# Differences of the second product beside the first one, ScalarE's parametric ReLU for the leak

## The chip, the cores and the metric

One core of a Trainium2 chip runs the whole program. The metric is the device time of one execution in microseconds (us). In the profile PE is TensorE's matmul, PEld its weight load, DVE is VectorE, ACT is ScalarE, POOL is GpSimd, and SP is SyncE, whose queue issues most DMAs.

## The reference

```python
def _attn_ref(q, k, v, p):
    # sm_attn: softmax(scale * q k^T) v
    p_packed = sm_attn(p, k, v)
    return sm_attn(q, p_packed, p_packed)
...
def _moe_ref(x, w_gate, w_val, w_out, rms_g):
    rms = np.sqrt(np.mean(x * x, axis=-1, keepdims=True) + 1e-06)
    xn = x / rms * rms_g
    g = xn @ w_gate
    silu = g * (1.0 / (1.0 + np.exp(-g)))
    return (silu * (xn @ w_val)) @ w_out
...
def _moe2_ref(x, w_in, w_out):
    h = x @ w_in
    g = np.maximum(0.01 * h, h)
    return g @ w_out
```

The three run one after the other: 8 x 8 heads of 576 x 64 with 32 packed rows; then 4608 tokens of 512, first through the gated layer (1536 wide), then through the leaky one (2048 wide). The change touches only the leaky layer.

## The kernel before

All matmuls are fp32-accurate by splitting each operand into a high and a low part: ACT copies the high part (`act_copy`), DVE subtracts it from the value for the low part (`sub`, L167), and `mm3` runs hi x hi, lo x hi and hi x lo. So a product of two operands has three matmuls, and each operand costs one ACT and one DVE instruction to split.

**The z stage.** The first 2048 tokens of the leaky layer are computed beside the second half of the attention, in 64 steps: `stage3z` multiplies by `w_in` into PSUM (`zh`), ACT makes 0.01 x h (`zr`), DVE takes the maximum (`zgf`, L1095), ACT and DVE split the result (`zgh`, `zgl`), and two steps later `stage4z` multiplies by `w_out`. `fold` (L895, `pwps`) is a small product in between, whose weights `w` come by DMA.

**The last stage.** The other 2560 tokens go through the leaky layer in three passes of 2 x 448, 2 x 448 and 2 x 384 tokens (`HALF`). Each of the two matrix products is cut 2 x 2 and done with seven products in place of eight, i in `ORDER` = (1, 5, 6, 2, 7, 3, 4). A pass p has 56 steps of the first product (`h_part`: 8 column blocks j, the seven i inside) and then 56 of the second (`o_part`: seven i, the eight j inside). Below, h0, o0, h1, o1, h2 and o2 are these six half passes. Each step takes one 256 KB piece of weights (`pc`) and issues six matmuls. `load_piece` runs once per step on SP's queue, over a ring of `sum(RING)` buffers, so that many steps ahead; a buffer is free again when its step is done.

Around these matmuls the other engines do the following.
- `joins` adds the seven products together: ACT copies two of them out of PSUM (b1, b5), DVE adds the others from PSUM to b1, b6, b7, and two adds whose operands both lie in SBUF (`b6<-b6,b5` and `b5<-b7,b5`, L1483) run on POOL, in the h and in the o half. h has eight PSUM banks in rotation.
- `leak` turns each of the four results of a j into g11, g12, g21, g22: an ACT copy times 0.01 (`r`) and a DVE maximum (L1476).
- `g_split` splits the operands of the second product, 56 in a pass, into `gh` and `gl`. For i = 5, 6, 7, 4 the operand is a difference, made in place on POOL (`mix`, L1539), 32 in a pass: g12-g11 after the split for i = 1, g22-g11 after the one for i = 5, g22-g12 and g21-g11 after the one for i = 6. The first split is issued at step 50 of a pass (`SPLIT0`), and `GBUFS` = 5 buffers are in rotation.
- `load_ys` (L1149) brings the inputs of the next pass at step 60, into the `yl` tiles, which the h half has just used; `mix_ys` (L1154) makes four differences of them on POOL (`yx`), and `split_ys` cuts the seven operands, two parts each, on ACT and DVE, all in the o half.
- `out_part` transposes the four results of the second product on DVE (L1558) into two output tiles `ob`, and stores each with 8 DMAs (4 in the last pass's second tile) on SP's queue, in the last pass every second one on ACT's.

A scheduler sets the order of instructions on each engine from the order of the code; each engine then runs its own in order.

Of the kernel before, what the change touches and what calls it, by code (L numbers as in the profile page):

```python
# [67 lines left out]
def pack_attention_moe_kernel(  # L68
# [1065 lines left out]
    def y_tiles(p):  # L1134
        for i in ORDER:
            for x in "hl":
                yt[p, i, x] = bw0.tile([P, 2, WMAX], F32R, tag=f"y{x}{i}", bufs=1, name=f"y{x}{i}{p}")
# [5 lines left out]
    def load_ys(p):  # L1143
        if p < len(HALF):
            y_tiles(p)
            at, n = HALF[p]
            for i, k_, c in ((1, 0, 0), (7, 0, 1), (3, 2, 1), (2, 2, 0)):
                t0 = at + c * n
                nc.sync.dma_start(out=y_raw(p, i), in_=y_dram[:, k_ : k_ + 2, t0 : t0 + n])  # L1149
# [13 lines left out]
    def ys_work(p):  # L1163
        if p >= len(HALF):
            return []
        mix = {i: [lambda i=i: mix_ys(p, i)] for i in (5, 6, 7, 4)}
        cut = {i: [lambda i=i, k_=k_: split_ys(p, i, k_) for k_ in range(2)] for i in ORDER}
        todo = mix[5] + mix[6] + cut[1] + mix[4] + cut[5] + cut[6] + mix[7]
        return todo + cut[2] + cut[3] + cut[4] + cut[7]
# [475 lines left out]
```

## Time and profile before

| | |
|---|---|
| runs, median (lowest to highest) | 1695.46 us (1692.63 to 1696.5) |
| the profiled execution | 1692.93 us |
| its span, from first to last instruction | 1691.1 us |
| mean granted clock of TensorE | 0.978 |
| busy: PE, DVE, ACT, POOL | 1600.1, 1164.3, 721.9, 649.9 us |

The span is what the trace covers; the 1.8 us between it and the profiled execution's time lie outside. Busy shares are means over stages with different limits: the last stage takes the last 447 us of the span, the z stage lies in the middle.

### The profile page before, as it was taken

The numbers are of one execution on the slowest core, as the hardware profiler recorded it, in microseconds if no ns is written. First come the engines' busy times: TensorE is split into PE (matmuls) and PEld (weight loads), VectorE is DVE, ScalarE is ACT, GpSimd is POOL, SyncE is SP. The second block draws the span as 40 slices with busy tenths as digits, with TensorE's granted clock in tenths as the row PEclk, the third lists the DMA queues.
The fourth block names the chain that finished last, engine by engine and source line by source line (L and its number), as shares of the span: only waits on it lengthen the run. The fifth ranks groups of instructions, "written<-read, shape, count | busy, mean of one in ns | idle before, by whom it ended". The sixth has DMA issues, their size and how long they took to land.

```text
span 1691.1 us, 27956 instructions
## 1 busy us (share of the span) xinstructions
PE 1600.1 (95%) x10410; PEld 1411.3 (83%) x10410; DVE 1164.3 (69%) x1878; ACT 721.9 (43%) x1332; POOL 649.9 (38%) x462
## 2 busy tenths in 40 slices
PE   6789999999999999999998999999999799979998
PEld 4578889888988778888877999999999689959997
DVE  7888985877477776676433566635557976697686
ACT  3465454544245544454323433442223433444343
POOL 1243344533212241312123655632235833481572
PEclk8899999999999999999999999999999899989999
DMA  9645542668186545723157666832057558747975
GB/s 282 211 152 180 166 137 100 249 217 295 56 292 225 162 160 187 238 83 90 54 169 278 243 216 232 323 138 73 26 202 220 176 174 256 240 126 215 294 238 156
DMA packets 170903, 318.52 MB, mean 188 GB/s; under 512 B 18192, under 2 KB 82704, under 8 KB 167696
## 3 DMA queue, kind: packets, MB, share of 16 engines
q1 hardware_dynamic: 169136, 315.95, 57.0%
q8 instruction: 83, 1.36, 0.3%
q10 hardware_dynamic: 1632, 0.79, 0.2%
q14 instruction: 52, 0.43, 0.1%
HBM read 245.11 MB, written 71.57 MB: 187 GB/s over the span
## 4 chain that ended last, share of the span: by engine, by line
PE 74%; DVE 11%; DMA 7%; issue 3%; ACT 2%; SPq 1%; POOL 1%; DVEq 0%; ACTq 0%; POOLq 0%
PE y L142 16%; PE h L142 11%; PE o L142 10%; PE g L142 8%; PE v L142 8%; PE zh L142 7%; PE zo L142 6%; PE pwps L895 3%; DMA w<-in_moe_w_in_dram 1%; DMA k<-in_k_dram 1%; DVE yl L167 1%; DVE gl L167 1%; PE s L142 1%; DMA w<-in_moe_w_out_dram 1%; DVE cvw L722 1%
## 5 line engine op out<-in xcount | busy, mean ns | idle before, releaser
L142 PE MATMUL y<-hh,wo 128*128 128x288 f32 x1536 | 268.7, 297 | 9.0 <-DVE pw L167 8.1
L167 POOL TENSOR_TENSOR hl<-sg,hh 128x576 fp32r<-128x576 f32 x96 | 146.8, 1529 | 317.5 <-ACT hh L159 310.3
L142 PEld LDWEIGHTS y<-hh,wo 128*128 128x128 f32 x1536 | 225.3, 189 | 17.0 <-DVE pw L167 9.3
L950 DVE TENSOR_TENSOR y_acc<-y_acc,y 128x288 f32<-128x288 f32 x320 | 142.2, 449 | 134.6 <-PE y L142 134.6
L142 PE MATMUL o<-gh,pc 128*128 128x448 f32 (+1 forms) x672 | 180.4, 367 | 0.0
L142 PE MATMUL zo<-w,zgh 128*128 128x512 f32 x512 | 171.9, 393 | 0.0
L167 DVE TENSOR_TENSOR gl<-g,gh 128x448 fp32r<-128x448 f32 (+1 forms) x168 | 148.6, 922 | 27.4 <-ACT gh L159 23.3
L142 PE MATMUL y<-hl,wo 128*128 128x288 f32 x768 | 166.1, 296 | 0.0
L142 PE MATMUL zh<-zyh,w 128*128 128x512 f32 x512 | 162.9, 394 | 1.5 <-DVE y_acc L950 1.5
L142 PE MATMUL h<-yh,pc 128*128 128x448 f32 (+1 forms) x672 | 159.1, 357 | 0.5 <-DVE y_acc L950 0.5
L142 PE MATMUL g<-ath,pw 128*128 128x288 f32 x768 | 147.8, 303 | 6.6 <-DVE pw L167 2.6
L142 PEld LDWEIGHTS g<-ath,pw 128*128 128x128 f32 x768 | 114.8, 188 | 41.6 <-ACT hh L159 14.2
L1539 POOL TENSOR_TENSOR g<-g,g 128x448 f32<-128x448 f32 (+1 forms) x96 | 131.9, 1394 | 42.4 <-DVE g L1476 27.3
L142 PE MATMUL o<-gl,pc 128*128 128x448 f32 (+1 forms) x336 | 117.4, 382 | 28.3 <-DVE gl L167 28.3
L142 PE MATMUL v<-ath,pw 128*128 128x288 f32 x768 | 144.0, 297 | 0.0
L159 ACT ACTIVATE gh<-g 128x448 fp32r<-128x448 f32 (+1 forms) x168 | 92.7, 559 | 116.5 <-PE o L142 69.9
L142 PEld LDWEIGHTS o<-gh,pc 128*128 128x128 f32 x672 | 130.1, 196 | 8.3
L142 PEld LDWEIGHTS h<-yh,pc 128*128 128x128 f32 x672 | 123.9, 188 | 9.0 <-DVE y_acc L950 0.8
L142 PEld LDWEIGHTS y<-hl,wo 128*128 128x128 f32 x768 | 124.6, 189 | 3.4 <-issue 2.5
L159 ACT ACTIVATE hh<-sg 128x576 fp32r<-128x576 f32 x96 | 65.5, 683 | 137.1 <-DVE sg L927 129.2
L142 PEld LDWEIGHTS v<-ath,pw 128*128 128x128 f32 x768 | 115.5, 188 | 1.5 <-DVE sn L477 0.8
L142 PEld LDWEIGHTS zh<-zyh,w 128*128 128x128 f32 x512 | 95.3, 188 | 22.7 <-issue 2.5
(198 smaller groups left out, 3247.9 us busy)
## 6 DMA issues: line engine op xcount, KB each, us to landing
pc<-s_dram SPq DMA_DIRECT2D x192, 256.0 KB
pc<-w_dram SPq DMA_DIRECT2D x144, 256.0 KB
w<-w_dram SPq DMA_DIRECT2D x76, 256.0 KB
wo<-wo_dram SPq DMA_DIRECT2D x36, 512.0 KB
w_dram<-w2s SPq DMA_DIRECT2D x32, 512.0 KB
w<-w_dram SPq DMA_DIRECT2D x16, 1024.0 KB
s_dram<-ss SPq DMA_DIRECT2D x32, 512.0 KB
v<-in_v_dram SPq DMA_DIRECT2D x16, 576.0 KB
```

What stands on the lines that cost most here:

```text
L142: mm = nc.tensor.matmul(ps, lhsT=lh if a == "h" else ll, rhs=rh if b == "h" else rl, start=start and i == 0, stop=stop and i == n - 1,)
L159: nc.scalar.activation(out=o, in_=i, func=AF.Copy, scale=scale)
L167: eng.tensor_tensor(out=o, in0=a, in1=hi.bitcast(F32), op=ALU.subtract)
L722: nc.vector.scalar_tensor_tensor(out=cu, in0=low, scalar=29, in1=cu, op0=ALU.logical_shift_right, op1=ALU.bitwise_or,)
L895: nc.tensor.matmul(ps[32 * h : 32 * h + 32], lhsT=lpw[2 * (n // NFG) + bb][rs, 2 * u + h // 2, c : c + 32], rhs=w[h // 2][rs], start=True, ...
L950: pace[:] = [nc.vector.tensor_tensor(out=ya, in0=ya, in1=pv, op=ALU.add).ins]
L1539: nc.gpsimd.tensor_tensor(out=o, in0=a, in1=b, op=ALU.subtract)
```

## The change

1. The leak is one ACT instruction, a parametric ReLU with slope 0.01 (`AF.Prelu`), in the last stage and in the z stage, in place of an ACT copy and a DVE maximum.
2. Of the 32 differences of a pass, 16 (g12-g11 and g22-g12) are made in `leak` when g12 is there, still on POOL, beside the first product. The other 16 (g22-g11 and g21-g11, after the splits for i = 5 and i = 6) are DVE's, beside the second one. The joins' two SBUF adds of the o half are DVE's too.
3. The eight splits of i = 1 are made in `leak` when g11 is there; the others eight steps ahead. `GBUFS` is 9, the ring of pieces has 10 buffers in place of 15.
4. The inputs of the next pass are loaded at step 4 of the h half into the output tiles, which the o half needs only later; their differences on POOL are paced behind the join of i = 2 in the h half. The 14 cuts are in the code after step 56.
5. In the last pass the last eight steps run all matmuls of one half of the output columns (q = 0) before those of the other, and the two halves of the tokens change places, so that the last tile stored is one of 4 DMAs.

```diff
-RING = (9, 6)
-GBUFS = 5
-RBUFS = 2
-SPLIT0 = 50
+RING = (9, 1)
+GBUFS = 9
+CUT = 3
...
-        r = zwg.tile([P, 512], F32, tag="r", bufs=2, name=f"zr{s_}{m}")
-        act_copy(r, ps, scale=0.01)
         gf = zwg.tile([P, 512], F32, tag="gf", bufs=2, name=f"zgf{s_}{m}")
-        pace[:] = [nc.vector.tensor_tensor(out=gf, in0=r, in1=ps, op=ALU.max).ins]
+        pace[:] = [nc.scalar.activation(out=gf, in_=ps, func=AF.Prelu, alpha=0.01).ins]
...
+    def start(p, c):
+        at, n = HALF[p]
+        return at + (c ^ (p == len(HALF) - 1)) * n
+
+    def load_ys(p):
+        if p >= len(HALF):
+            return
+        at, n = HALF[p]
+        if p == 0:
+            for i in ORDER:
+                y_tiles(p, i)
+        else:
+            for c in range(2):
+                t = out_tile(p, c).rearrange("p b m j -> p (b m j)")
+                for k_, i in ((0, (1, 7)[c]), (1, (2, 3)[c])):
+                    t_ = t[:, k_ * 2 * WMAX : (k_ + 1) * 2 * WMAX]
+                    yt[p, i] = t_.rearrange("p (k n) -> p k n", k=2)
+        for i, k_, c in ((1, 0, 0), (7, 0, 1), (3, 2, 1), (2, 2, 0)):
+            t0 = start(p, c)
+            nc.sync.dma_start(out=y_raw(p, i), in_=y_dram[:, k_ : k_ + 2, t0 : t0 + n])
+
+    def y_tiles(p, i):
+        for x in "hl":
+            yt[p, i, x] = bw0.tile([P, 2, WMAX], F32R, tag=f"y{x}{i}", bufs=1, name=f"y{x}{i}{p}")
+
+    def out_tile(p, c):
+        return bw.tile([P, WMAX // T, 4, T], F32, tag=f"ob{c}", bufs=1, name=f"ob{p}{c}")
...
-        yt[p, i] = bw0.tile([P, 2, WMAX], F32, tag="yx", bufs=3, name=f"yx{i}{p}")
+        if i != 7 or p == 0:
+            yt[p, i] = bw0.tile([P, 2, WMAX], F32, tag="yx", bufs=3, name=f"yx{i}{p}")
         nc.gpsimd.tensor_tensor(out=y_raw(p, i), in0=a, in1=b, op=ALU.subtract)
 
     def split_ys(p, i, k_):
         n = HALF[p][1]
+        if (p, i, "h") not in yt:
+            y_tiles(p, i)
...
         n = HALF[p][1]
-        r = bw.tile([P, WMAX], F32, tag="r", bufs=RBUFS, name=f"r{p}{name}{j}")[:, :n]
-        act_copy(r, c, scale=0.01)
         g = bw.tile([P, WMAX], F32, tag=f"g{name}{j}", bufs=1, name=f"g{name}{j}{p}")[:, :n]
-        nc.vector.tensor_tensor(out=g, in0=r, in1=c, op=ALU.max)
+        nc.scalar.activation(out=g, in_=c, func=AF.Prelu, alpha=0.01)
         gt[p, name, j] = g
-
-    def joins(st, i, ps, n, at, done):
+        if name == 11:
+            g_split(p, j)
+        if name == 12:
+            g11, g22 = gt[p, 11, j], gt[p, 22, j]
+            mix(nc.gpsimd, g11, g, g11)
+            mix(nc.gpsimd, g, g22, g)
+
+    def mix(eng, o, a, b):
+        eng.tensor_tensor(out=o, in0=a, in1=b, op=ALU.subtract)
...
-            into(st[1], ps, st[1])
+            pace[:] = [into(st[1], ps, st[1]).ins]
             done(11, st[1])
-            into(st[6], st[6], st[5], nc.gpsimd)
-            into(st[5], st[7], st[5], nc.gpsimd)
+            into(st[6], st[6], st[5], eng)
+            into(st[5], st[7], st[5], eng)
             done(22, st[5])
...
-        joins(hb.setdefault((p, j), {}), i, ps, n, f"h{p}{j}", done)
+        joins(hb.setdefault((p, j), {}), i, ps, n, f"h{p}{j}", done, nc.gpsimd)
...
-        g11, g12, g21, g22 = (gt[p, x, j] for x in (11, 12, 21, 22))
-
-        def mix(o, a, b):
-            nc.gpsimd.tensor_tensor(out=o, in0=a, in1=b, op=ALU.subtract)
-
-        if i == 1:
-            mix(g11, g12, g11)
-        elif i == 5:
-            mix(g11, g22, g11)
+        g11, g21, g22 = (gt.get((p, x, j)) for x in (11, 21, 22))
+        if i == 5:
+            mix(nc.vector, g11, g22, g11)
         elif i == 6:
-            mix(g12, g22, g12)
-            mix(g11, g21, g11)
+            mix(nc.vector, g11, g21, g11)
...
-        k0 = at // T + c * nb
+        k0 = start(p, c) // T
...
-        t = pieces.pop(at).rearrange("p (h x) -> p h x", h=2)
-        for q, st in enumerate(ob_):
+        last = p == len(HALF) - 1 and i == ORDER[-1]
+        at0 = at - j if last and j == 7 else at
+        if last and j < 7:
+            return
+        todo = [(q, at_) for q in range(2) for at_ in range(at0, at + 1)]
+        for q, at_ in todo:
+            j = at_ - at0 if last else j
+            st = ob_[q]
+            t = pieces[at_].rearrange("p (h x) -> p h x", h=2)
...
-                joins(st, i, st["ps"], n, f"o{p}{q}", lambda name, c, q=q: out_part(p, name, q, c))
+                done = lambda name, c, q=q: out_part(p, name, q, c)
+                joins(st, i, st["ps"], n, f"o{p}{q}", done, nc.vector)
+        for at_ in range(at0, at + 1):
+            pieces.pop(at_)
...
-    ahead, later = [], []
+    def paced(f_):
+        with tc.issue_after(pace[0]):
+            f_()
+
+    later = []
     for at, (p, stage, i, j) in enumerate(SEQ):
-        if at % 112 == SPLIT0:
-            ahead += [lambda p=p, k_=k_: g_split(p, k_) for k_ in range(56)]
-        if at % 112 == 60:
+        k_ = at % 112
+        if k_ == 4:
+            load_ys(p + 1)
+            later += mixes(p + 1)
+        if 12 <= k_ < 48 and k_ % 8 == 4 and later:
+            paced(later.pop(0))
+        if k_ == 56:
             assert not later
-            load_ys(p + 1)
-            later += ys_work(p + 1)
-        if at % 112 > 62 and at % 2 and later:
+            later += cuts(p + 1, (1, 7, 2, 3, 5, 6, 4))
+        if k_ > 56 and k_ % CUT == 0 and later:
             later.pop(0)()
-        if ahead:
-            ahead.pop(0)()
+        if k_ >= 56 and k_ - 56 + 8 < 56:
+            g_split(p, k_ - 56 + 8)
         (o_part if stage else h_part)(p, *((i, j) if stage else (j, i)), at)
         load_piece()
-    assert not ahead and not later and not pieces
+    while later:
+        later.pop(0)()
+    assert not later and not pieces
```

On POOL, at the end of h0's differences and from there to the joins of h1, the rows before are these (a name is the tile, the pass and the block, behind it a number of the instance):

```order
L1539 TENSOR_TENSOR g1150_14060<-g2150_14105,g1150_14060 128x448
L1539 TENSOR_TENSOR g1160_14152<-g2160_14197,g1160_14152 128x448
L1539 TENSOR_TENSOR g1170_14259<-g2170_14319,g1170_14259 128x448
L1483 TENSOR_TENSOR b6o00_14682<-b6o00_14682,b5o00_14568 128x448
L1483 TENSOR_TENSOR b6o01_14687<-b6o01_14687,b5o01_14573 128x448
L1483 TENSOR_TENSOR b5o00_14568<-b7o00_14903,b5o00_14568 128x448
L1483 TENSOR_TENSOR b5o01_14573<-b7o01_14912,b5o01_14573 128x448
L1483 TENSOR_TENSOR b6h10_15146<-b6h10_15146,b5h10_15135 128x448
```

And the rows from the last join of h0 to those of h1 in the changed kernel:

```order
L1510 TENSOR_TENSOR b5h07_14080<-b7h07_14118,b5h07_14080 128x448
L1504 TENSOR_TENSOR g1170_14103<-g1270_14134,g1170_14103 128x448
L1504 TENSOR_TENSOR g1270_14134<-g2270_14122,g1270_14134 128x448
L1510 TENSOR_TENSOR b6h10_14945<-b6h10_14945,b5h10_14934 128x448
L1510 TENSOR_TENSOR b5h10_14934<-b7h10_14978,b5h10_14934 128x448
L1504 TENSOR_TENSOR g1101_14957<-g1201_14994,g1101_14957 128x448
```

The four adds of o0 (`b6o`, `b5o`) and the differences in front of them are gone from POOL; the join of h1 (`b6h10`) comes straight behind the last differences of h0.

On DVE, at the border of h0 and o0, the rows before, from a leak of the last block to the tenth split of o0:

```order
L1476 TENSOR_TENSOR g1270_14300<-r0127_14298,b6h07_14240 128x448
L167 TENSOR_TENSOR gl05_14305<-g1150_14060,gh05_14304 128x448
L167 TENSOR_TENSOR gl06_14324<-g1160_14152,gh06_14323 128x448
L1476 TENSOR_TENSOR g2170_14319<-r0217_14317,b7h07_14275 128x448
L167 TENSOR_TENSOR gl07_14339<-g1170_14259,gh07_14338 128x448
L167 TENSOR_TENSOR yl11_14378<-yl11_14378,yh11_14377 128x448 x2
L167 TENSOR_TENSOR yl51_14380<-yx51_14434,yh51_14379 128x448 x2
L167 TENSOR_TENSOR gl08_14352<-g1100_13600,gh08_14351 128x448
L167 TENSOR_TENSOR gl09_14365<-g1110_13692,gh09_14364 128x448
```

And the changed kernel's, from the last block's join for i = 3 to the first difference on DVE:

```order
L1510 TENSOR_TENSOR b6h07_14091<-h073_14126,b6h07_14091 128x448
L166 TENSOR_TENSOR yl31_14429<-ob11_13469,yh31_14428 128x448
L166 TENSOR_TENSOR yl41_14676<-yx41_13891,yh41_14675 128x448
L1510 TENSOR_TENSOR b7h07_14118<-h074_14140,b7h07_14118 128x448
L166 TENSOR_TENSOR yl41_14676<-yx41_13891,yh41_14675 128x448
L166 TENSOR_TENSOR gl07_14106<-g1170_14103,gh07_14105 128x448
L166 TENSOR_TENSOR gl08_14153<-g1100_13460,gh08_14152 128x448
L166 TENSOR_TENSOR gl09_14172<-g1110_13556,gh09_14171 128x448
L166 TENSOR_TENSOR gl010_14185<-g1120_13648,gh010_14184 128x448
L166 TENSOR_TENSOR gl011_14198<-g1130_13740,gh011_14197 128x448
L1504 TENSOR_TENSOR g1100_13460<-g2200_13485,g1100_13460 128x448
```

The cuts of pass 1's inputs (`yl..`) stood among the splits of o0 and stand now ahead of `gl07`, the last split of i = 1. The two last cuts (`yl41`) overwrite the tile that the last step of h0 reads. The difference `g1100` was POOL's.

On SP's queue, at the border of o0 and h1, the rows before:

```order
L1272 DMA pc126_15115<-w1_dram_63 128x2x256
L1272 DMA pc127_15126<-s1_dram_65 128x512
L1569 DMA out_0_dram<-ob00_14793 32x8x128 x4
L1569 DMA out_0_dram<-ob00_14793 32x6x128 x4
L1272 DMA pc128_15137<-s1_dram_65 128x512
```

And the changed kernel's at the same border, which has the two tiles' stores around the loads of pass 2's inputs:

```order
L1292 DMA pc119_14886<-w1_dram_63 128x2x256
L1292 DMA pc120_14894<-s1_dram_65 128x512
L1150 DMA ob21_14966<-y_dram_60 128x2x384
L1292 DMA pc121_14914<-s1_dram_65 128x512
L1150 DMA ob21_14966<-y_dram_60 128x2x384
L1292 DMA pc122_14925<-w1_dram_63 128x2x256
L1589 DMA out_0_dram<-ob00_14602 32x8x128 x4
L1589 DMA out_0_dram<-ob00_14602 32x6x128 x4
```

The loads of the inputs stood amid the pieces 64 to 70 and go now into the tile `ob` of which the store stands a few rows ahead; the first one comes when nine of h1's pieces (112 to 120) have been issued.

## Rows read from the trace of the kernel before

**Rows 1.** The page: busy time by engine, and the chain that ended last.

```profile
PE 1600.1 (95%) x10410; PEld 1411.3 (83%) x10410; DVE 1164.3 (69%) x1878; ACT 721.9 (43%) x1332; POOL 649.9 (38%) x462
...
PE 74%; DVE 11%; DMA 7%; issue 3%; ACT 2%; SPq 1%; POOL 1%; DVEq 0%; ACTq 0%; POOLq 0%
```

**Rows 2.** Windows: h0, o0, h1, o1, h2, o2, and a stretch of the z stage.

```profile
core 0: us, PE busy (x) PEld busy (x) DVE busy (x) ACT busy (x) POOL busy (x), PEclk, DMA share, GB/s
1244.10:1313.20 69.10, 69.09 (x335) 63.03 (x336) 47.77 (x71) 26.07 (x52) 33.38 (x26) 1.00 0.80 249
1313.20:1405.30 92.10, 76.10 (x340) 67.84 (x339) 76.31 (x86) 37.12 (x70) 50.70 (x31) 0.91 0.58 175
1405.30:1474.30 69.00, 69.00 (x335) 62.75 (x335) 50.73 (x76) 26.08 (x52) 33.51 (x26) 1.00 0.79 248
1474.30:1562.60 88.30, 76.01 (x339) 66.99 (x339) 76.40 (x86) 37.05 (x70) 47.44 (x31) 0.92 0.60 179
1562.60:1620.90 58.30, 58.30 (x335) 58.28 (x335) 40.21 (x76) 22.59 (x50) 28.71 (x25) 1.00 0.89 284
1620.90:1683.00 62.10, 62.10 (x338) 57.50 (x336) 54.47 (x71) 29.39 (x58) 34.24 (x28) 1.00 0.67 197
...
480.00:840.00 360.00, 356.55 (x2056) 297.08 (x2055) 250.92 (x413) 179.57 (x337) 85.20 (x59) 1.00 0.50 164
```

**Rows 3.** Waits of PE over the span: us in total, times, longest.

```profile
PE o L142 <- DVE gl L167: 28.3, 11, 5.8
...
PE pwps L895 <- DMA w<-w_dram: 2.7, 1, 2.7
```

**Rows 4.** Timeline at the start of o0, VectorE and GpSimd.

```profile
1317.09 0.63 DVE L1476 TENSOR_TENSOR g<-r,b5h 128x448 f32<-128x448 f32 x1 [1.25 <-ACT r L159]
...
1317.40 2.30 POOL L1154 TENSOR_TENSOR yx<-yl,yl 128x896 f32<-128x896 f32 x1 [3.11 <-DMA yl<-y_dram]
...
1317.63 2.55 DVE L1476 TENSOR_TENSOR g<-r,b6h 128x448 f32<-128x448 f32 x1
```

**Rows 5.** Groups by form in 1475 to 1513 (o1): busy us, mean ns.

```profile
L167 DVE TENSOR_TENSOR gl<-g,gh 128x448 fp32r<-128x448 f32 x13 | 15.4, 1222 | 0.0
...
L1539 POOL TENSOR_TENSOR g<-g,g 128x448 f32<-128x448 f32 x15 | 21.7, 1462 | 5.8 <-DVE gl L167 5.8
```

**Rows 6.** VectorE's timeline late in o0, the first row beside POOL's adds.

```profile
1386.36 5.75 DVE L167 TENSOR_TENSOR gl<-g,gh 128x448 fp32r<-128x448 f32 x4
...
1393.10 0.63 DVE L1558 STREAM_TRANSPOSE ob<-b5o 128x448 f32<-128x448 f32 x1
1393.65 1.65 DVE L167 TENSOR_TENSOR gl<-g,gh 128x448 fp32r<-128x448 f32 x3
```

**Rows 7.** Groups by form in h1 (1405 to 1475).

```profile
L1539 POOL TENSOR_TENSOR g<-g,g 128x448 f32<-128x448 f32 x10 | 12.9, 1288 | 9.8 <-DVE g L1476 9.4
L1483 POOL TENSOR_TENSOR b6h<-b6h,b5h 128x448 f32<-128x448 f32 x8 | 11.0, 1370 | 38.7 <-DVE b7h L1483 32.7 <-ACT yh L159 6.0
...
L159 ACT ACTIVATE r<-b1h 128x448 f32<-128x448 f32 x8 | 4.6, 576 | 17.2 <-DVE b1h L1483 17.2
L1483 DVE TENSOR_TENSOR b1h<-h,b1h 128x448 f32<-128x448 f32 x8 | 5.0, 625 | 2.3 <-PE h L142 1.8
```

**Rows 8.** Short windows: columns as in Rows 2.

```profile
1410.00:1415.00 5.00, 5.00 (x26) 4.55 (x25) 3.17 (x5) 1.16 (x2) 2.82 (x2) 1.00 1.06 317
1415.00:1420.00 5.00, 5.00 (x26) 4.53 (x26) 4.45 (x7) 2.52 (x6) 2.57 (x2) 1.00 1.00 352
...
1488.00:1499.00 11.00, 6.59 (x19) 5.00 (x19) 11.00 (x9) 3.54 (x7) 9.95 (x6) 0.68 0.23 72
```

**Rows 9.** SP's timeline at the border of o0 and h1.

```profile
1397.77 0.33 SPq L1272 DMA_DIRECT2D pc<-s_dram  x1
1398.19 5.89 SPq L1569 DMA_DIRECT2D out_dram<-ob  x8
```

**Rows 10.** Links of the chain of waits that are DMAs.

```profile
857.99 6.38 DMA out_dram<-zob
...
865.27 5.31 DMA w<-w_dram
...
1310.31 5.15 DMA yl<-y_dram
```

**Rows 11.** Timeline of the end, after the last matmul.

```profile
1682.97 1.02 DVE L1483 TENSOR_TENSOR b7o<-o,b7o 128x384 f32<-128x384 f32 x2 [3.12 <-PE o L142]
1683.90 1.03 DVE L1558 STREAM_TRANSPOSE ob<-b7o 128x384 f32<-128x384 f32 x2
1684.96 2.48 ACTq L1569 DMA_DIRECT2D out_dram<-ob  x4
```

More of the change, by code (lines that the diff above doesn't have):

```diff
@@ L1132, in pack_attention_moe_kernel @@
     yt = {}
[L1134 to L1137, printed above, removed]
+    def start(p, c):
[22 more added lines that the diff above has]
+        return bw.tile([P, WMAX // T, 4, T], F32, tag=f"ob{c}", bufs=1, name=f"ob{p}{c}")
     def y_raw(p, i):
@@ L1141, in y_raw @@
         return yt[p, i][:, :, :n] if (p, i) in yt else yt[p, i, "l"][:, :, :n].bitcast(F32)
[L1143 to L1149, printed above, removed]
     def mix_ys(p, i):
         a, b = [y_raw(p, x) for x in {5: (7, 1), 6: (3, 5), 7: (3, 7), 4: (2, 6)}[i]]
-        yt[p, i] = bw0.tile([P, 2, WMAX], F32, tag="yx", bufs=3, name=f"yx{i}{p}")
+        if i != 7 or p == 0:
+            yt[p, i] = bw0.tile([P, 2, WMAX], F32, tag="yx", bufs=3, name=f"yx{i}{p}")
         nc.gpsimd.tensor_tensor(out=y_raw(p, i), in0=a, in1=b, op=ALU.subtract)
@@ L1161, in split_ys, with mixes, cuts, ys_work @@
         sub(nc.vector, yt[p, i, "l"][:, k_, :n], r, h)
-    def ys_work(p):
+    def mixes(p):
+        return [lambda i=i: mix_ys(p, i) for i in (5, 6, 7, 4)] if p < len(HALF) else []
+    def cuts(p, order):
         if p >= len(HALF):
             return []
[L1166 to L1169, printed above, removed]
+        return [lambda i=i, k_=k_: split_ys(p, i, k_) for i in order for k_ in range(2)]
+    def ys_work(p):
+        m, c = mixes(p), {i: cuts(p, (i,)) for i in ORDER}
+        todo = m[:2] + c[1] + m[3:] + c[5] + c[6] + m[2:3]
+        return todo + c[2] + c[3] + c[4] + c[7]
     sq_ = {}
@@ L1472, in leak, with joins @@
         n = HALF[p][1]
-        r = bw.tile([P, WMAX], F32, tag="r", bufs=RBUFS, name=f"r{p}{name}{j}")[:, :n]
-        act_copy(r, c, scale=0.01)
         g = bw.tile([P, WMAX], F32, tag=f"g{name}{j}", bufs=1, name=f"g{name}{j}{p}")[:, :n]
-        nc.vector.tensor_tensor(out=g, in0=r, in1=c, op=ALU.max)
+        nc.scalar.activation(out=g, in_=c, func=AF.Prelu, alpha=0.01)
         gt[p, name, j] = g
-    def joins(st, i, ps, n, at, done):
+        if name == 11:
[6 more added lines that the diff above has]
+        eng.tensor_tensor(out=o, in0=a, in1=b, op=ALU.subtract)
+    def joins(st, i, ps, n, at, done, eng):
         ps = ps[:, :n]
         def into(o, a, b, eng=nc.vector):
-            eng.tensor_tensor(out=o, in0=a, in1=b, op=ALU.add)
+            return eng.tensor_tensor(out=o, in0=a, in1=b, op=ALU.add)
         if i in (1, 5, 6, 7):
@@ L1555, in out_part @@
         if (p, c) not in obs:
-            obs[p, c] = bw.tile([P, WMAX // T, 4, T], F32, tag=f"ob{c}", bufs=1, name=f"ob{p}{c}"), []
+            obs[p, c] = out_tile(p, c), []
         ob, done = obs[p, c]
```

## The prediction

> **What bounds the kernel now.** The page comes first [rows 1]. PE is busy for 1600.1 of 1691.1 us, and the chain that ended last is PE for 74%, but DVE for 11%. So PE bounds the kernel, and somewhere DVE does. The windows say where [rows 2]. The z stage is bound by PE: in its 360 us PE is idle for 3.5. In the last stage a pass runs the same 336 matmuls in its h half and in its o half, with moving operands of the same width, so that PE needs the same time for both. It takes 69.10, 69.00 and 58.30 us in h, at a granted clock of 1.00, but 92.10, 88.30 and 62.10 in o. The three o halves are 23.0, 19.3 and 3.8 us too long, 46.1 us in sum.
>
> The waits name the cause: the matmuls of o wait for the low part `gl` of their operand for 28.3 us [rows 3]. That is less than 46.1, since PE also loses speed after it stood still: the granted clock of o0 and o1 is 0.91 and 0.92 [rows 2], and 0.68 in a stretch of o1 in which PE was busy for 6.6 of 11 us [rows 8], that is, between the 1.2 and 2.4 GHz levels. Both parts go if the waits go.
>
> Why is `gl` late? DVE executes only 86 instructions in o0, yet is busy for 76.31 us [rows 2], 0.89 us each. The timeline shows what stretches them. A DVE instruction with two SBUF operands takes 0.63 us with POOL idle, and 2.55 us when a POOL instruction of 2.30 us has begun 0.23 us before it [rows 4]. In the worst part of o1, `gl` takes 1222 ns on average, beside POOL's differences of 1462 ns [rows 5]. Late in o0, four `gl` take 5.75 us beside POOL's adds, but three take 1.65 us, 0.55 each, when POOL is silent [rows 6]. So o is bound by DVE, and DVE by POOL.
>
> The Trainium skill says the same more strictly (SBUF — State Buffer, section "SBUF: two separate sides"): the port pair that DVE and GpSimd share is an exclusive lock, and whoever comes second is blocked for the other's whole instruction. The 2.55 us agree with that. By it POOL's work beside h would cost DVE as much for each instruction as that beside o did, which speaks for the second rival below.
>
> **o halves, -46.1 us.** By the order of rows POOL has nothing left between the last differences of h0 and the first join of h1. What DVE has to do in a 448 pass is 48 `gl`, 16 differences, 14 joins and 8 transposes, 86 instructions. At 0.55 us without POOL [rows 6], and at most 0.63 [rows 4, 6], that is 47 to 54 us of the 69 that PE needs. The tightest part is i = 5 and i = 6, with one `gl` and one difference per step: 1.10 us against 69.1/56 = 1.23 us for PE. The bursts at the end of an i (for i = 7 two joins from PSUM, four adds and two to four transposes, some 5 us) lie inside a lead of eight steps, 9.9 us. ACT has one `gh` per step, 0.58 us by the nearest row [rows 7]. So o comes down to the length of h. Bounds of this term: -46.1 if nothing is left, -36 if in passes 0 and 1 every second of the 32 DVE instructions of the i = 5 and 6 parts still loses 0.3 us (2 x 16 x 0.3 = 9.6). I take -46.1 and price the leftovers by place.
>
> **Start of o, +1 (0 to 4).** The 14 cuts of the next inputs, on ACT and DVE, stand around the joins of the last block and ahead of `gl07`. After the last h matmul DVE still has one join, two cuts and `gl07`, each with an ACT copy in front of it: about 4 us. POOL's two last differences (1.29 us each [rows 7]) can hold two of them up, 6.6 us at most. `gl07` is needed in the eighth step, 8.6 us after the start. So it should be in time; half a microsecond for each of the two passes that cut, and 2 us each as the upper end.
>
> **h halves, +2 (0 to 6).** DVE keeps 40 joins from PSUM at 0.625 us [rows 7] and has 22 instructions with two SBUF operands (eight `gl`, 14 cuts) at 0.55: 37 us, and 66 if each is held up by a whole POOL difference of 1.3, still under 69. ACT has seven instructions per block, 7 x 0.576 = 4.0 of 8.6 us. I price the parametric ReLU as the plain copy, 0.58 us [rows 7]. The trace shows no such function; ACT would bound h only if one took over 1.7 us. POOL gets fuller: four instructions of 1.29 to 1.37 us per block, 43 us in 69, and four differences of the inputs at 2.30 us [rows 4], 52 in all. The join `b6h` waits behind these. An input difference, two g differences and its own add are 6.3 us, while PSUM's eight banks let PE run ahead by 8 x 1.23 = 9.9 us. So mostly hidden; I allow 1 us for each of the passes 0 and 1, and 3 us as the upper end, since two input differences and two more may stand in front of one join.
>
> **Pieces at the start of h1 and h2, +2 (0 to 9).** The ring falls from 15 to 10 pieces, a lead of 12.3 us. A transfer takes some 5.2 us from issue to use [rows 10], so 7 us of slack are left. SP's queue eats into these. One output tile takes 5.89 us of issue time [rows 9], two of them stand within 25 steps, and the new load of inputs must wait until the first tile has landed, some 5 us after its issue, with pieces 121 and on queued behind it. Counting in steps (piece n is issued when step n - 10 is done), pieces 123 to 125 are issued about 4 steps, 5 us, ahead of their use: just enough. The bytes are tight too. In the first 25 us of h1 there are 20 pieces, 5.3 MB, two output tiles, 1.84 MB, and inputs of 1.57 MB: 8.7 MB, 350 GB/s. The trace has 317 and 352 GB/s in such stretches [rows 8], and 284 as a mean of h2 without a wait [rows 2]. I take 1 us for each start. The upper end is all of it at 284 GB/s: 30.8 in place of 25 us for h1, and 8.1 MB (no inputs, faster steps) in 28.6 us for h2, 5.8 + 3.6 = 9.4 us.
>
> The Trainium skill has a rule against this part (DMA: Bandwidth & Descriptors, section "Specifications"): HBM gives a core about 358 GB/s. By it 8.7 MB take 24.4 us, an estimate, and the start of h1 would just fit. The trace's best row is 352 over 5 us, so it neither reaches nor breaks that figure.
>
> **The end, -1.8 (-2.5 to 0).** After the last matmul there now follow two joins of 1.02 us together, two transposes of 1.03, and 8 DMA issues on two queues, 4 on each in 2.48 us [rows 11]. With q = 0 first, one join and one transpose remain, -1.0, and of a tile with four DMAs two per queue, -1.2. The larger DMAs may take 0.3 longer to land.
>
> **z stage, 0 (-3 to +4).** The maximum goes to ACT, which has 360 - 180 us free [rows 2]. PE waits hardly at all here, so nothing is gained. The scheduler moves the product `pwps` of one `fold` some 4.5 us earlier on PE (19 matmuls of 512 columns, at 69.1/336 us for 448 columns). It waits 2.7 us for its weights already [rows 3]; these were queued on SP behind a load that waited for a store of 6.38 us [rows 10]. In the new order that load stands behind the weights, which so come about 4 us earlier as well. The two cancel; if the store still stands in the way, +4.5.
>
> **Sum.** 1692.93 (the profiled execution, 1.8 above its span) - 46.1 + 1 + 2 + 2 - 1.8 + 0 = 1650.0 us. The median of the runs shown is 2.5 above that execution, so the forecast for a median is 1652.5, and I say 1652.
>
> **Rivals.**
> - *Pieces come late at the pass starts* (the upper end of that term). For it: the ring is a third shorter, stores and loads now block SP's queue in the same stretch. Against it: in h, where pieces are used at the same rate, PE is busy without a gap before [rows 2]. It gives 1652 + 7 = 1659, up to 1662 if the start of o0 has its 2 us as well. Chance 0.15.
> - *POOL hurts beside h.* The 16 moved differences and the input differences stretch DVE and the joins until the banks run out, and the cuts come late for `gl07`: 4 + 6 in place of 1 + 2, +7, 1659. For it: POOL goes from 33 to 52 us of 69 there. Against it: DVE has 47.8 us there, less than before once the maxima are gone, and its joins from PSUM take 625 ns even in the busy h1 [rows 7]. Chance 0.10.
> - *The fold in z waits longer*: +4.5, 1656.5. Chance 0.05; it lies in the likeliest one's range.
> - *Slower: the ring of ten is too short throughout.* Place: every step of all six half passes. If a piece needs L us from the issue to its use, ten steps take L and not 12.3 once L is above that; the 43 us are lost when 336/10 x (L - 12.3) = 43, at L = 13.6. At 14.5 it would be 1652 + 74 = 1726. The landings of 5.2 us [rows 10] speak against it. Chance 0.02.
> - That the change doesn't do what it says is no rival: the rows of the order show POOL empty beside o.
>
> The likeliest, DVE alone in o with small leftovers, 1644 to 1657, has 0.68. The range 1643 to 1663 takes in the first three rivals and most of what is between. A change under 0.2% (3.4 us) couldn't be told from none; for that nearly all of the 46 us would have to come back, which only the slower rival does: 0.96 faster, 0.02 the same, 0.02 slower.
>
> **What would show it.** Right: o0 and o1 of 69 to 71 us at a clock near 1.00, `gl` at 0.55 us, no wait of PE for `gl` over 1 us, POOL empty in o and at some 50 us in h. The parametric ReLU at about 0.6 us. Wrong: o halves still over 75 us; waits of PE for a `pc` DMA in the first 20 us of h1 or h2; waits for PSUM banks behind `b6h` in h; a longer wait of `pwps` for its weights.

## The result and the profile after

The changed kernel takes 1648.97 us, the median of four runs (1646.48 to 1649.72), the kernel before 1695.98: a ratio of 0.9723, with a 95% interval of 0.9706 to 0.9741. The forecast was 1652, with a range of 1643 to 1663. The profiled execution took 1646.48 us.

First the page of the changed kernel: busy time by engine, and the chain that ended last.

```profile
PE 1582.8 (96%) x10410; PEld 1405.6 (85%) x10410; DVE 1028.8 (63%) x1778; ACT 725.5 (44%) x1332; POOL 562.1 (34%) x402
...
PE 85%; DVE 6%; DMA 6%; issue 1%; ACT 1%; SPq 1%; POOL 0%; DVEq 0%; ACTq 0%; POOLq 0%
```

PE runs the same 10410 matmuls, but its share of the chain went from 74% [rows 1] to 85%, and DVE's from 11% to 6%. The windows show where, h0, o0, h1, o1, h2, o2, then the end, the first 25 us of h1, and a stretch of the z stage (columns as in [rows 2]).

```profile
1244.10:1313.30 69.20, 69.18 (x336) 63.12 (x337) 33.33 (x52) 32.14 (x63) 43.30 (x33) 1.00 0.81 250
1313.30:1382.00 68.70, 68.70 (x338) 63.09 (x337) 53.31 (x94) 31.34 (x60) 10.55 (x4) 1.00 0.73 209
1382.00:1451.40 69.40, 69.40 (x337) 63.09 (x337) 36.99 (x57) 32.26 (x65) 41.70 (x33) 1.00 0.84 267
1451.40:1520.00 68.60, 68.60 (x337) 62.99 (x337) 52.51 (x93) 31.51 (x58) 7.45 (x4) 1.00 0.75 213
1520.00:1578.40 58.40, 58.40 (x338) 58.38 (x337) 28.99 (x51) 25.12 (x54) 31.96 (x29) 1.00 0.90 285
1578.40:1636.80 58.40, 58.40 (x338) 58.31 (x336) 44.02 (x86) 27.44 (x54) 3.77 (x4) 1.00 0.76 232
1636.80:1644.70 7.90, 0.23 (x2) 0.00 (x0) 1.14 (x2) 0.00 (x0) 0.00 (x0) 0.77 0.51 101
...
1382.00:1407.00 25.00, 25.00 (x122) 22.73 (x122) 10.58 (x18) 8.03 (x15) 11.57 (x9) 1.00 1.04 350
...
480.00:840.00 360.00, 360.00 (x2081) 301.78 (x2080) 221.85 (x360) 184.52 (x343) 88.11 (x60) 1.00 0.51 167
```

Against [rows 2], o0, o1 and o2 went from 92.10, 88.30 and 62.10 us to 68.7, 68.6 and 58.4, the h halves stayed, and the clock of o0 and o1 is 1.00. DVE executes 94 instructions in o0 in 53.31 us, 0.57 each, where 86 took 76.31.

POOL is not quite empty in o0: its last four instructions of h0 run there, 10.55 us. Two of them are differences of g, which take 1.29 us each at [rows 7]. Here, beside a row of DVE instructions without a gap, they take 7.99 (start us, us):

```profile
1320.92 7.99 POOL L1504 TENSOR_TENSOR g<-g,g 128x448 f32<-128x448 f32 x2 [4.91 <-ACT gh L158]
```

The chain through the last stage is now PE from end to end (start us, us, what):

```profile
1313.56 68.63 PE o L141 x336
1382.19 69.41 PE h L141 x336
1451.60 68.63 PE o L141 x336
1520.22 58.40 PE h L141 x336
1578.63 58.42 PE o L141 x336
1637.05 0.02 issue
1637.07 0.57 DVE b7o L1510
```

From the first product of h0 to the join behind the last product (in the kernel before the first of two) the kernel before took 438.9 us (1244.11 to 1682.97), the changed one 393.0 (1244.12 to 1637.07): 45.9 us. From there to the end of the span it was 8.1 us and is 7.6. That is the whole 46.4 us between the two spans. Ahead of h0 the two traces agree to 0.01 us, but by chance: the z stage, from its first product to its last, is 3.2 us shorter (476.6 to 895.8 before, 479.3 to 895.3 after), and the first matmul of the first layer came 1.5 us later in this run (76.3 and 77.8 us).

The parametric ReLU costs ACT what the copy cost. From the groups by form (1200 to 1645 us, and the z stage):

```profile
L1494 ACT ACTIVATE g<-b1h 128x448 f32<-128x448 f32 x16 | 9.2, 577 | 24.8 <-DVE b1h L1510 22.7 <-DMA pc<-s_dram 2.1
...
L1092 ACT ACTIVATE zgf<-zh 128x512 f32<-128x512 f32 x57 | 34.0, 596 | 54.6 <-PE zh L141 54.3
```

### The profile page after: what moved, and what is told of

It is laid out like the page before. It is cut to its first block, busy times and chain, and to the rows that moved or that the text cites. A ratio compares the mean times of both kernels' runs of the same rounds, so it can differ in the third digit from the quotient of the medians.

```text
span 1644.7 us, 27726 instructions
## 1 busy us (share of the span) xinstructions
PE 1582.8 (96%) x10410; PEld 1405.6 (85%) x10410; DVE 1028.8 (63%) x1778; ACT 725.5 (44%) x1332; POOL 562.1 (34%) x402
## 3 DMA queue, kind: packets, MB, share of 16 engines
q1 hardware_dynamic: 169136, 315.95, 58.6%
## 4 chain that ended last, share of the span: by engine, by line
PE 85%; DVE 6%; DMA 6%; issue 1%; ACT 1%; SPq 1%; POOL 0%; DVEq 0%; ACTq 0%; POOLq 0%
PE y L141 16%; PE h L141 12%; PE o L141 12%; PE zh L141 10%; PE zo L141 10%; PE g L141 8%; PE v L141 8%; PE pwps L894 3%; PE s L141 2%; DMA wo<-in_moe_w_out_dram 1%; PE xp L141 1%; DMA k<-in_k_dram 1%; DMA sl<-w_dram 1%; PE s L469 1%; PE ms L583 1%
## 5 line engine op out<-in xcount | busy, mean ns | idle before, releaser
L141 PE MATMUL o<-gh,pc 128*128 128x448 f32 (+1 forms) x672 | 184.9, 356 | 0.0
L141 PEld LDWEIGHTS o<-gh,pc 128*128 128x128 f32 x672 | 124.6, 188 | 7.2
L166 DVE TENSOR_TENSOR gl<-g,gh 128x448 fp32r<-128x448 f32 (+1 forms) x168 | 105.4, 641 | 28.3 <-ACT gh L158 24.5
L141 PEld LDWEIGHTS zo<-w,zgh 128*128 128x128 f32 x512 | 95.8, 188 | 19.1
```

The lines of the kernel that those rows point to most:

```text
L141: mm = nc.tensor.matmul(ps, lhsT=lh if a == "h" else ll, rhs=rh if b == "h" else rl, start=start and i == 0, stop=stop and i == n - 1,)
L166: eng.tensor_tensor(out=o, in0=a, in1=hi.bitcast(F32), op=ALU.subtract)
```

## The experiments

What precedes h0 moves by some microseconds between traces: over these kernels h0 starts between 1241.4 and 1246.5 us. The table therefore gives, beside the medians, the last stage alone, from its first product to the join behind its last product (the first of two, where two stand there), and the three o halves, all from one trace each. Each ratio is to the kernel before as it was timed beside that kernel. These medians of the kernel before were 1696.0, 1696.1, 1696.5 and 1694.0 us, so two kernels' medians can differ by some 2 us without a cause in the kernels. The o halves of `lead_pool` run into the h halves, so they are left out.

| kernel | median us | ratio to before (95%) | last stage us | o0, o1, o2 us |
|---|---|---|---|---|
| before | 1695.98 | 1 | 438.9 | 92, 88, 62 |
| changed | 1648.97 | 0.9706 to 0.9741 | 393.0 | 68.6, 68.6, 58.6 |
| `after_again` | 1649.39 | 0.9715 to 0.9747 | 393.0 | 68.6, 68.6, 58.6 |
| `prelu_only` | 1688.15 | 0.9939 to 0.9967 | 435.3 | 91, 87, 60 |
| `pool_diff` | 1646.31 | 0.9678 to 0.9727 | 394.5 | 68.9, 69.6, 58.6 |
| `pool_joins` | 1645.91 | 0.9670 to 0.9727 | 392.9 | 68.6, 68.6, 58.6 |
| `pool_dummy` | 1674.55 | 0.9843 to 0.9906 | 420.2 | 78.3, 85.8, 58.6 |
| `lead_pool` | 1659.88 | 0.9771 to 0.9809 | 405.6 | |
| `late_ys` | 1663.83 | 0.9788 to 0.9836 | 407.3 | 77.2, 74.5, 58.6 |
| `ring8` | 1649.48 | 0.9707 to 0.9742 | 399.0 | 68.6, 68.6, 58.7 |
| `ring8_again` | 1650.35 | 0.9724 to 0.9754 | 396.6 | 68.6, 68.6, 58.7 |
| `ring6` | 1662.91 | 0.9784 to 0.9821 | 406.8 | 71.5, 71.2, 59.2 |
| `copy_max` | 1663.12 | 0.9796 to 0.9847 | 408.3 | 75.5, 75.5, 58.6 |
| `tail8` | 1648.01 | 0.9709 to 0.9742 | 393.2 | 68.6, 68.6, 58.6 |

**The parametric ReLU alone**, in the kernel before.

```diff
...
-        r = bw.tile([P, WMAX], F32, tag="r", bufs=RBUFS, name=f"r{p}{name}{j}")[:, :n]
-        act_copy(r, c, scale=0.01)
...
-        nc.vector.tensor_tensor(out=g, in0=r, in1=c, op=ALU.max)
+        nc.scalar.activation(out=g, in_=c, func=AF.Prelu, alpha=0.01)
```

> The kernel before with the parametric ReLU alone, in both stages; every difference, add, load and cut stays where it was. Theory (POOL beside the o halves makes DVE late): the maxima that go away lie almost all in the h halves, which are bound by PE, so o0, o1 and o2 stay near 92, 88 and 62 us, at most some 5 us shorter in all because three late maxima at the border of h and o are gone: 1690 to 1696 us. Rival (DVE's own load is what was too much, and 160 instructions fewer is the gain): half of the gain or more, under 1673 us.

Measured: 1688.15 us, 2 below the range given, and in the trace a last stage 3.6 us shorter and a z stage of 416.5 in place of 419.2, for which the expectation had nothing. 160 DVE instructions less leave o0 at 91 us. This is a weak test of DVE's own load, since only 4 of them lay in o0 (82 instructions there, 86 before). What speaks against that load is the changed kernel's 94 instructions in 53.31 us.

**The differences, or the adds, of o back on POOL.**

```diff
-            mix(nc.vector, g11, g22, g11)
+            mix(nc.gpsimd, g11, g22, g11)
...
-            mix(nc.vector, g11, g21, g11)
+            mix(nc.gpsimd, g11, g21, g11)
```

> The changed kernel with the 16 differences of each o half back on POOL; all else as changed. Theory: in the parts i = 5 and i = 6 a step costs DVE one low part (0.55 us) plus the hold by one POOL difference (1.3 to 1.46 us), about 1.9 us against PE's 1.23, over 16 steps 11 us late less a lead of some 6 us: 4 to 7 us per pass, 1660 to 1670 us. Rival (DVE's own load): DVE has 48 instructions fewer, so no loss, 1647 to 1650 us.

```diff
-                joins(st, i, st["ps"], n, f"o{p}{q}", done, nc.vector)
+                joins(st, i, st["ps"], n, f"o{p}{q}", done, nc.gpsimd)
```

> The changed kernel with the four SBUF adds of each o half back on POOL, the differences stay on DVE. Theory: four adds of 1.3 us hold DVE for some 5 us once per pass, which the lead of eight steps (9.9 us) covers: 0 to 2 us longer, 1648 to 1651 us. Rival (any POOL work beside o costs its whole time, since DVE is close to its limit): 3 x 5 us, 1662 us or more.

Measured: no loss in the medians; the last stage is 394.5 and 392.9 us, against 393.0. For the joins the theory held; for the differences even its lower end was 14 us too high. So the step from "POOL beside o" to "late" was too short. The timeline of `pool_diff` in o0, POOL and then DVE, shows why:

```profile
1318.62 27.79 POOL L1504 TENSOR_TENSOR g<-g,g 128x448 f32<-128x448 f32 x17 [4.90 <-ACT gh L158]
...
1332.10 1.33 DVE L166 TENSOR_TENSOR gl<-g,gh 128x448 fp32r<-128x448 f32 x1 [0.17 <-PE o L141]
1333.59 1.33 DVE L166 TENSOR_TENSOR gl<-g,gh 128x448 fp32r<-128x448 f32 x1 [0.17 <-ACT gh L158]
1335.08 1.33 DVE L166 TENSOR_TENSOR gl<-g,gh 128x448 fp32r<-128x448 f32 x1 [0.16 <-ACT gh L158]
1336.58 12.35 DVE L166 TENSOR_TENSOR gl<-g,gh 128x448 fp32r<-128x448 f32 x9 [0.17 <-ACT gh L158]
```

POOL's 17 differences run without a gap, and between the starts of two `gl` lie 1.49 us: one DVE instruction passes per POOL instruction. In the single rows the data have a part in it, since each `gh`, and `gl` behind it, also waits 0.9 us for the difference that POOL has just made. In the last row nine `gl` go at the same pace without a wait. The hold takes the place of DVE's 0.55 us, it isn't added, as I had reckoned; [rows 6] had shown that already, with four `gl` in 5.75 us beside POOL's adds, 1.44 each. Against PE's 1.23 us a step the splits lose 0.26 us, 4 us in 16 steps, and the lead of eight steps covers that.

**POOL work that no data depend on.**

```diff
...
+        if stage and i in (5, 6):
+            if i == 5 and j == 0:
+                spare = bw0.tile([P, 2, WMAX], F32, tag="yx", bufs=3, name=f"spare{p}")
+                nc.gpsimd.memset(spare, 0.0)
+            d_ = spare[:, 0, : HALF[p][1]]
+            with tc.issue_after(gs_last[0]):
+                nc.gpsimd.tensor_tensor(out=d_, in0=d_, in1=d_, op=ALU.subtract)
```

> The changed kernel with 16 more POOL subtractions in each o half, one per step of i = 5 and i = 6, on a spare tile that nothing else reads, each issued behind a low part's split; no data depend on them. Theory (the port, not the data, makes DVE late): a step costs DVE 1.10 us plus up to 1.3 us of hold against PE's 1.23; 16 steps make it 15 to 19 us late less a lead of 6: 8 to 12 us per pass, 1670 to 1685 us. Rival (POOL was a slow link in a chain of data): nothing waits for these instructions, so 1648 to 1651 us.

Measured: 1674.55 us, within what the theory gave, and by dose. The scheduler put the 16 subtractions meant for o2 into o1 too: o0 with 16 of them is 9.7 us longer, o1 with 32 is 17.2 longer, o2 with none is not. DVE, then POOL, in o0:

```profile
1328.24 1.35 DVE L1504 TENSOR_TENSOR g<-g,g 128x448 f32<-128x448 f32 x1
1329.52 1.35 DVE L1562 TENSOR_TENSOR gl<-g,gh 128x448 fp32r<-128x448 f32 x1
1330.79 1.35 DVE L1504 TENSOR_TENSOR g<-g,g 128x448 f32<-128x448 f32 x1
...
1327.80 14.04 POOL L1651 TENSOR_TENSOR spare<-spare 128x448 f32<-128x448 f32 x11
```

Again one DVE instruction per POOL instruction, here 1.27 us. But a step now needs two of them from DVE, 2.54 us against 1.23. This shows the hold itself, apart from data, and that here it costs by the number of DVE instructions that a step needs while POOL runs.

**Parts 2 and 3 undone together** (lead and differences).

```diff
-GBUFS = 9
+GBUFS = 5
...
-        if name == 11:
-            g_split(p, j)
-        if name == 12:
-            g11, g22 = gt[p, 11, j], gt[p, 22, j]
-            mix(nc.gpsimd, g11, g, g11)
-            mix(nc.gpsimd, g, g22, g)
...
-        if i == 5:
-            mix(nc.vector, g11, g22, g11)
...
+        if i == 1:
+            mix(nc.gpsimd, g11, g12, g11)
+        elif i == 5:
+            mix(nc.gpsimd, g11, g22, g11)
         elif i == 6:
-            mix(nc.vector, g11, g21, g11)
+            mix(nc.gpsimd, g12, g22, g12)
+            mix(nc.gpsimd, g11, g21, g11)
...
-        if k_ >= 56 and k_ - 56 + 8 < 56:
-            g_split(p, k_ - 56 + 8)
+        if k_ == 50:
+            ahead += [lambda p=p, x=x: g_split(p, x) for x in range(56)]
+        if ahead:
+            ahead.pop(0)()
```

> The changed kernel with part 3 undone and the differences as before: 5 buffers for gh and gl, the first split six steps ahead of the o half, all differences on POOL behind their splits (the scheduler then leaves 22 to 24 of 32 in the o half). The inputs, their differences and cuts stay where the change put them. The run pool_diff showed DVE making one gl per POOL difference, 1.49 us, with no loss. Theory (rate against lead): 22 differences in a row give one gl per 1.49 us for 33 us, 0.26 us per step slower than PE, 6 us in all, and the lead is 5 steps, 6 us, of which the cuts at the border have taken some 4: 2 to 6 us per pass, 1655 to 1667 us. Rival (the inputs' differences and cuts in o were the whole trouble): 1647 to 1650 us.

Measured: the last stage is 12.6 us longer, 5.6, 5.3 and 1.7 us in the three passes, where 2 to 6 each were given. POOL runs 22 differences in a row at 1.53 us, and DVE's splits go at that pace, five in 7.28 us:

```profile
1317.76 33.76 POOL L1498 TENSOR_TENSOR g<-g,g 128x448 f32<-128x448 f32 x22 [4.84 <-DVE gl L166]
...
1340.63 7.28 DVE L166 TENSOR_TENSOR gl<-g,gh 128x448 fp32r<-128x448 f32 x5 [0.16 <-ACT gh L158]
```

Two things limit the splits here. In front of these five, ACT's `gh` waits for POOL's differences, 11.6 us in all in o0; the five themselves go without a wait for data, held by POOL. The run shows the loss, but does not part the hold from POOL as a slow link in the chain of data.

**Part 4 undone** (inputs, their differences and cuts in o).

```diff
...
-        if k_ == 4:
-            load_ys(p + 1)
-            later += mixes(p + 1)
-        if 12 <= k_ < 48 and k_ % 8 == 4 and later:
-            paced(later.pop(0))
-        if k_ == 56:
+        if k_ == 60:
             assert not later
-            later += cuts(p + 1, (1, 7, 2, 3, 5, 6, 4))
-        if k_ > 56 and k_ % CUT == 0 and later:
+            load_ys(p + 1)
+            later += ys_work(p + 1) if p + 1 < len(HALF) else []
+        if k_ > 62 and at % 2 and later:
             later.pop(0)()
```

> The changed kernel with part 4 undone: the inputs of the next pass are loaded at step 60 into their own tiles, so that their four differences (POOL, 2.3 us each) and 14 cuts (DVE and ACT) lie in the o half again; differences of g, lead of eight steps and ring as changed. Theory (rate against lead): in i = 5 and i = 6 DVE has 16 low parts, 16 differences, 14 cuts, 46 x 0.55 = 25 us, and up to 9 us of hold by POOL, 31 to 34 us against 20 us of PE and a lead of 9.9: 1 to 5 us for each of passes 0 and 1, 1651 to 1659 us. Rival (POOL must be silent in o, else most of the loss comes back): 1670 us or more.

Measured: 14.4 us longer in the last stage, 8.5 in o0 and 5.8 in o1, more than the 1 to 5 each that I gave. For o0 I had left out the other direction of the hold. POOL and DVE in o0, then ACT and PE:

```profile
1331.55 9.36 POOL L1159 TENSOR_TENSOR yx<-yl,yl 128x896 f32<-128x896 f32 x1 [3.78 <-DVE yl L166]
...
1337.82 0.61 DVE L1496 TENSOR_TENSOR g<-g,g 128x448 f32<-128x448 f32 x1
1338.36 0.61 DVE L166 TENSOR_TENSOR yl<-yx,yh 128x448 fp32r<-128x448 f32 x1
1340.94 1.16 DVE L166 TENSOR_TENSOR yl<-yl,yh 128x448 fp32r<-128x448 f32 x2 [1.97 <-POOL yx L1159]
...
1340.94 1.04 ACT L158 ACTIVATE yh<-yx 128x448 fp32r<-128x448 f32 x2 [10.90 <-POOL yx L1159]
...
1342.69 1.11 PE L141 MATMUL o<-gl,pc 128*128 128x448 f32 x2 [3.39 <-DVE gl L166]
```

POOL's last input difference, 2.3 us long at [rows 4], takes 9.36: DVE's instructions follow each other without a gap, one per 0.54 us, and it ends only after they have stopped. ACT, which cuts its result, stands still for 10.90 us, with the next high parts behind that cut in its queue, and DVE for 1.97; PE then waits for 3.39. That is not the whole of it. In o1 no input difference takes over 2.3 us, and 5.8 us are lost all the same, with waits of PE of 1.22 and 1.99 us. Why the lead did not cover these stays open.

**Shorter rings**, 8 and 6 pieces.

```diff
-RING = (9, 1)
+RING = (7, 1)
```

> The changed kernel with a ring of 8 pieces. In its trace the store of the second tile holds SP's queue from 1386.5 to 1392.0 us, and the next piece, 123, is issued 3.5 us ahead of its use without a wait. With a ring two shorter that store stands two pieces earlier, and the first piece behind it is issued some 1 us ahead of its use. Theory (the queue behind the stores is the limit): about 2 us lost at each start of h1 and h2, 1651 to 1654 us. Rival (a ring is long enough while it is longer than a transfer, 5 us against 8 x 1.23): 1647 to 1650 us.

> The changed kernel with a ring of 6 pieces. By the same count the first piece behind the second tile's store is issued 1.5 us after PE wants it, so PE waits some 4 to 5 us at each start of h1 and h2, and the first tile's store costs some as well: 1657 to 1665 us. Rival (6 x 1.23 = 7.4 us is still longer than a transfer): 1647 to 1650 us.

> The ring of 8 once more: its trace had a last stage of 399.0 us, 6.0 longer than the changed kernel's 393.0, with waits for pieces, but its median was only 0.5 us above. Theory: the loss is real and the start of that run was an early one; the median is 3 to 6 us above that of after_again, the last stage 397 to 400 us. Rival: the waits were an accident of the traced run; median within 2 us of after_again.

Measured: `ring6` loses 13.9 us in the median, within the range given, but not where it was counted. PE's waits for pieces lie in all six halves: 1.55 us in h0, 2.02 and 2.07 in the last steps of o0 and o1, 1.09 and 1.79 in h1 and h2, 0.84 at the end of o2.

```profile
PE o L141 <- DMA pc<-w_dram: 4.9, 3, 2.1
PE h L141 <- DMA pc<-w_dram: 4.4, 3, 1.8
```

With 8 pieces the traces show the loss at its place, 6.0 and 3.6 us in the last stage, but the medians are only 0.5 and 1.0 us above the changed kernel's, which can't be told from none; both forecasts of a median were too high. In both traces h0 started at 1241.6 and 1242.1, two to five us earlier than in the two of the changed kernel (1244.1 and 1246.2); why stays open. Waits of PE in `ring8`:

```profile
PE h L141 <- DMA pc<-s_dram: 3.0, 3, 1.7
```

So by the traces ten pieces are just enough, and eight are not quite. The margin is in SP's queue (timeline of the changed kernel at the border of o0 and h1):

```profile
1374.41 6.51 SPq L1589 DMA_DIRECT2D out_dram<-ob  x8
...
1386.52 5.47 SPq L1589 DMA_DIRECT2D out_dram<-ob  x8
1392.13 0.83 SPq L1292 DMA_DIRECT2D pc<-s_dram  x2
```

Piece 123, first behind the second store, is issued at 1392.1 and due at 1382.0 + 11 x 1.24 = 1395.6, 3.5 us later; PE didn't wait.

**The changed kernel again.**

> The changed kernel once more, beside the next three. Theory: what differs between executions lies ahead of the last stage: the first product of h0 has started between 1241.4 and 1246.5 us in ten traces, with the z stage at 416 to 417 us in every kernel with the parametric ReLU and 419.2 in the kernel before. So the last stage (first product to last join) is 393.0 us again within 0.5, whatever the total. Rival: the last stage itself varies by some us from run to run (pieces that land late at times), and is off by more than 2 us.

Measured: a last stage of 393.0 us for the second time, with h0 starting 2.1 us later than in the first trace. The last stage was the same, what precedes it was not.

**Copy and maximum back in the last stage**, the rest as changed.

```diff
-RING = (9, 1)
+RING = (8, 1)
...
-        nc.scalar.activation(out=g, in_=c, func=AF.Prelu, alpha=0.01)
+        r = bw.tile([P, WMAX], F32, tag="r", bufs=1, name=f"r{p}{name}{j}")[:, :n]
+        act_copy(r, c, scale=0.01)
+        nc.vector.tensor_tensor(out=g, in0=r, in1=c, op=ALU.max)
```

> The changed kernel with the leak of the last stage as before, an ACT copy and a DVE maximum (the z stage keeps the parametric ReLU; the ring has 9 pieces and the product's tile one buffer, for room). Theory: the 32 maxima of a pass lie in the h half, where DVE has 33 of 69 us of work; with up to 1.3 us each it stays under 69. Last stage 393 to 395 us, total 1648 to 1651. Rival (the parametric ReLU carries a part of the gain in the last stage, as the 3.6 us that it gave alone): 396 us or more.

Measured: a last stage of 408.3 us, so the theory fell and the rival's range held, though not for DVE's load in h. At the border DVE has the maxima of the last block in its queue behind the cuts, and one of them feeds the split for the first steps of o0. DVE, then PE:

```profile
1324.07 0.61 DVE L1496 TENSOR_TENSOR g<-r,b1h 128x448 f32<-128x448 f32 x1
1325.32 0.63 DVE L166 TENSOR_TENSOR gl<-g,gh 128x448 fp32r<-128x448 f32 x1 [0.64 <-ACT gh L158]
...
1325.34 1.86 PE L141 MATMUL o<-gh,pc 128*128 128x448 f32 x4 [4.80 <-ACT gh L158]
```

The maximum `g<-r,b1h` for `gl07` starts 12.3 us after o0's first product; PE waits for 4.8 us. The granted clock is 0.95 over the window 1313 to 1385, which takes in the wait. With the ReLU on ACT that link of the chain isn't in DVE's queue. The ring of 9 has a small part: PE waits 1.1 us for pieces in h1 and h2, and 13.8 of the 15.3 us lie in o0 and o1. The single buffer of `r` makes ACT stand still for 6.25 us ahead of this maximum, but DVE works without a gap from 1309.83 to 1324.68, so its queue and not the buffer made the maximum late. How the scheduler would have ordered that queue with two buffers was not run.

**The token halves of the last pass not exchanged.**

```diff
-        return at + (c ^ (p == len(HALF) - 1)) * n
+        return at + c * n
```

> The changed kernel with the halves of the tokens of the last pass not exchanged, so that the last tile goes out with eight DMAs of 96 KB and not four of 192 KB. From the last join's start to the end of the span the changed kernel takes 7.6 us, the kernel before 8.1. Theory (the end waits for 0.75 MB to be written, at some 200 GB/s, whatever the number of DMAs): 7.4 to 8.0 us. Rival (the issue of DMAs is the limit, 0.6 us each on two queues): two more per queue, 8.7 us or more.

Measured: from the last join's start (1638.85) to the end (1646.14) 7.29 us, just under the range given, and 7.63 in both traces of the changed kernel. In this one trace eight DMAs of 96 KB are 0.3 us quicker than four of 192 KB; the issues are not the limit. In the median, 1648.01 against 1648.97, that is not to be seen.

## Why the prediction was right

The place, the waiting engine and the size of the main term were right. The small terms came out 6.3 us lower in sum, and several reasons need mending.

- *o halves, -46.1.* Measured -23.4 and -19.7 by the windows, and -3.4 for o2 up to the last join (1637.07; the window ends at 1636.80). DVE's 53 us in o0 lie in the 47 to 54 forecast, but hold ten instructions that h0 left over, 7.7 us; the other 84 took 45.6. The 0.63 us that I read as "with POOL idle" at [rows 4] were not quite that, since POOL's instruction began 0.31 us into them; beside no POOL work a `gl` takes 0.61 us and the next starts 0.54 after it.
- *The reason behind that term.* "DVE is bound by POOL" was only half of it. By `pool_dummy` POOL's hold is real; by `pool_diff` and `pool_joins` POOL may work for 28 us beside o and cost nothing. While POOL has instructions in a row, what counts is how many DVE instructions a step needs (one per 1.3 to 1.5 us), times the steps, against the lead. The kernel before failed on all of these: some two dozen differences, the input differences of 2.3 us, 14 cuts in between, and a lead of five. Data were not what was late there: in o0 and o1 of the kernel before ACT's `gh` waits for none of POOL's differences; only its cuts wait for the input differences, 3.1 and 2.1 us, with `gh` behind them. Undoing parts 2 and 3 alone costs 12.6 us of the last stage, part 4 alone 14.4, and with all undone but the ReLU, as in `prelu_only`, it is 42.3 longer, more than the sum.
- *Start of o, +1*: 0. PE has no wait at either border, but it was closer than I had counted. After the last h matmul DVE had about eight cuts left and not two, and POOL's last two adds of h0 held some of them up. `gl07` was ready 7.4 us after the start of o0, where I had given 6.6 at most, and 1.2 us ahead of its step.
- *h halves, +2*: 69.2, 69.4 and 58.4 us, +0.6 in all. POOL's 43 us beside h hold nothing up; the second rival didn't come.
- *Pieces, +2*: 0, with 350 GB/s over the first 25 us of h1 as worked out. That stays under the 358 GB/s of the Trainium skill (DMA: Bandwidth & Descriptors, section "Specifications"), but the traces do not bear that figure out as a limit: over 20 us ahead of the last stage the changed kernel moved 403 GB/s (the row below, columns as in [rows 2]) and the kernel before 401, so the trace breaks it, though the rows that I had read did not. The 5.2 us from issue to use that I took from loads of inputs was too long for a piece, 3.5 were enough. The rival of late pieces was close: two buffers fewer show it in the trace, four in the median.

```profile
1087.00:1107.00 20.00, 19.58 (x155) 18.34 (x154) 7.04 (x10) 14.46 (x32) 11.38 (x7) 1.00 1.06 403
```

- *The end, -1.8*: -0.5. DVE's part came (2.05 to 1.15 us). The 1.2 us from fewer DMA issues did not, by `tail8`; the 0.3 us for larger DMAs did.
- *z stage, 0*: -3.2. I had put no price on DVE's 64 maxima there, since PE is nearly always busy [rows 2]; but the 3.5 us of idle time in it were waits for DVE and ACT, and they are gone: PE is busy for all of the 360 us from 480 to 840, and for 356.55 before. `prelu_only` shows -2.7 by the ReLU alone. The wait of `pwps`, which I had at 0 to +4.5, grew from 2.7 us [rows 3] to 4.2.

In sum 1650.0 was forecast for the profiled execution, and it took 1646.5: -0.4 in o, -1, -1.4 and -2 of leftovers that didn't come and -3.2 in z, against +1.3 at the end, make -6.7. The +2.7 us ahead of the z stage and +0.5 behind it bring that to -3.5; that the sum came out as close as this owes something to these chance differences.
